# Loading x by halves of the partitions and scoring one group of heads at a time, ahead of a mixture of experts on one core

## The chip, the cores and the metric

The kernel runs on one core of a Trainium2 chip. The metric is the time of one execution on the device in microseconds (us); smaller is better. The time before is the median of three executions.

## The reference

Two parts follow one another. The first is a cross attention between 512 tokens and 32 state rows, for 8 batches of 8 heads of width 64; the second is a mixture of 8 experts over the 544 rows of 512 numbers that each batch then has.

```python
scores = scale * np.matmul(x, state.transpose(0, 1, 3, 2))     # x (8,8,512,64), state (8,8,32,64)
a = softmax(scores);   xread = np.matmul(a, state)             # tokens read the states
scores2 = scale * np.matmul(state, x.transpose(0, 1, 3, 2))
a2 = softmax(scores2); sread = np.matmul(a2, x)                # states read the tokens
x = concatenate([xread, sread], axis=2)                        # then heads side by side: (8, 544, 512)
logits = x @ w_gate;  local_gate = sigmoid(x @ w_local)
# in a sequence, a row takes the expert of the row before it where local_gate >= 0.5,
# and its own best expert otherwise; the first row takes its own
h = np.maximum(x[b, s] @ w1[e], 0.0)                           # w1 (8, 512, 1024)
out[b, s] = p[e] * (h @ w2[e])                                 # w2 (8, 1024, 512), p the softmax of the logits
```

All numbers are float32.

## The kernel before, in words

The 512 tokens of a batch are one "unit", computed whole with the expert of the batch's first token; the state rows and the tokens that need another expert are done in small tiles beside it. A unit is two large products (w1, then w2). Each is taken as seven products of half-size blocks in place of eight (`seven`), so it needs sums of blocks: `first_sum` (`fs0` to `fs3`) adds quarters of w1 (tiles a11, a12, a21, a22), `column_sum` (`cs0` to `cs3`) adds quarters of the unit's tokens, `second_sum` adds quarters of w2 (tiles c). In the first product of a unit, block product 1 needs a11 and the tokens; product 5 is next and needs `fs0`, the sum of a21 and a22; product 6 needs `fs1`.

The attention of batches 0 and 1 runs ahead of the first unit, in the "head". The attention of batches 2 to 7 is cut into steps that are issued between the block products of the units, at numbered ticks (`FLOW`; the functions in `BESIDE` add the leftovers of batches 0 and 1, `GROUPS` the ticks of the routing). The order in the head is written out by hand in the string `HEAD`: one name after another is issued, each engine works its own instructions in that order, and an instruction that waits holds up all behind it on its engine.

A name is a step, a batch and, in most, a group of heads u (0 or 1: group 0 lies on partitions 0 to 63 of the transposed x, group 1 on partitions 64 to 127). The steps that matter here, with their engines:

- `sc` (`scores`, line 321, TensorE): the scores of a batch, eight products with one result bank for each group. `mx` (329, VectorE) is their maximum over the tokens, `nb` (333, GpSimd) its scaled negative, `et` (337, ScalarE) the exponents for the states' reads.
- `tr` (348, VectorE) turns the scores of a group in 32x32 blocks, `mo` (351, VectorE) is the maximum over the states, `sb` (358, GpSimd) subtracts it, `ex` (362, ScalarE) takes exponents, `zh` (369, GpSimd) and `zs` (372, VectorE) sum them, `zi` (377, VectorE) inverts, `ml` (381, GpSimd) multiplies, `tb` (385, VectorE) turns back.
- `tu`, `ec`, `sr`, `iv`, `st`, `rt`, `sl`, `sk`: the states' reads and their logits. `ga`, `gl`: the gates of the states.
- `lg` (436, TensorE) and `lt` (440, VectorE): the logits of the tokens of a batch. `fe` (547 to 553, VectorE): the first token's expert. `vv` (450, TensorE), `xr` and `xd` (459, 462): the tokens' reads, which are the unit's input.
- `kpN` issues N matmuls on zeros into a spare bank.

All loads go through one queue, SyncE's. Its order at the start is: x of batch 0, the other states, the gate weights, x of batch 1, then token-major x of batch 0 (`load_n`), the states again, `load_n` of batch 1, and x and `load_n` of batch 2. The transposed x of a batch is 1 MB in two loads of 512 KB (`load_t`, line 293); each brings two of the four k blocks of all 128 partitions:

```python
x = self.new(self.pools[b]["xp"], f"x_t{h}", (b,), [P, KT // 2, S])
self.nc.sync.dma_start(out=x..., in_=self.xt[b][:, h * D * 2:(h + 1) * D * 2])
```

`fe0` ends with `work.load(0, 0)` (line 839): SyncE waits there for the expert's number and then issues the four quarters of w1, 512 KB each, in the order a11, a21, a22, a12. The four quarters of w2 follow when the memory of the head is free.

Of the kernel before, what the change touches and what calls it, by code (L numbers as in the profile page):

```python
# [18 lines left out]
P = 128  # L19
B, H, S, N, DH = 8, 8, 512, 32, 64  # L20
D = H * DH
# [4 lines left out]
KT = D // P  # L26
FK = F // P
G = 2
# [75 lines left out]
class Banks:  # L104

    def __init__(self, tc, n):
        self.tc, self.ctx = tc, ExitStack()
        self.open(n)
# [8 lines left out]
class Slots:  # L117


    def __init__(self, pool):  # L120
# [17 lines left out]


HEAD = """  # L140
sc0 kp1 tr01 kp2 tr00 mo01 sc1 mo00 sb01 mx01 kp3 sb00 mx11 ex01 kp7 tr11 zh01 ex00 mx00 ga zs01 zh00 mx10 nb0 zi01
et01 zs00 ml01 tr10 et00 tu01 zi00 mo10 nb1 ml00 gl tb01 ec01 sb10 tu00 tb00 et10 mo11 lg0 ec00 sb11 lt0 et11 vv0 fe0
ex10 iv1 sr0 ex11 iv0 xd03 xr02 zh11 xr00 xd01 tu10 zh10 st0 zs11 tu11 zi11 ec10 cs0 ml11 zs10 ec11 zi10 rt0 sr1 ml10
tb11 sl0 st1 kp2 sk0 tb10 cs2 vv1 rt1 cs1 xr10 xr13 fs0 fs1
"""


BESIDE = """
1 lg1 lt1 cs3 fe1 fs3 fs2 xr12 / 2 ze / 3 xr11 / 4 sl1 sk1 / 6 wr12 wr13 / 7 wr10 wr11 / 8 ws0 / 10 ws1 / 11 wr00 wr01 /
12 wr02 wr03  # L150
"""


# [4 lines left out]
"""  # L158
FIRST, PERIOD = 2, 14
PER = 28  # L160
GROUPS = {(0, 2): (5, 8, 9, 11, 13, 14, 15), (2, 4): (57, 60, 61, 61, 64, 65, 67),
          (4, 8): (103, 105, 106, 107, 110, 111, 112)}
ONES = 18, 19, 21, 22, 24, 25, 27, 28, 29

# [1 line left out]
class Attention:  # L166


    def __init__(self, ctx, head, tc, xn, xt, st, stt, wgl, wgs, lt, xts, rows, work):
        nc = self.nc = tc.nc  # L170
        self.xn, self.xt, self.lt, self.xts, self.rows, self.work = xn, xt, lt, xts, rows, work
        self.wg, self.wh = wgs[:, 0], wgs[:, 1]
        self.ctx = ctx.enter_context(ExitStack())

        def pool(name, bufs, of=self.ctx, **more):
            return of.enter_context(tc.tile_pool(name=name, bufs=bufs, **more))

        right = dict(side="right")
        once = pool("once", 1, **right)
        self.tp, self.late = pool("tp", 1, **right), pool("late", 2, **right)  # L180
        self.sm = pool("sm", 3, **right)
        later = dict(xp=pool("xp", 1, **right), wk=pool("wk", 4, **right), tp=self.tp, late=self.late,
                     sp=pool("sp", 2, space=PSUM, **right))
        self.sp = later["sp"]
        self.p = pool("p", 3, space=PSUM, **right)
        first = dict(xp=pool("hx", 2, head), wk=pool("hw", 4, head), tp=pool("ht", 2, head), late=pool("hl", 2, head),
                     sp=later["sp"])
        second = dict(first, late=self.late, sp=pool("hs", 2, head, space=PSUM))
        self.pools = [first, second] + [later] * (B - 2)
        self.of = {}  # L190


        stt = stt.rearrange("p (b k n) -> p b k n", b=B, k=KT)
        self.sttc = [once.tile([P, n, KT, N], F32, name=f"sttc{i}") for i, n in enumerate((1, B - 1))]
        nc.scalar.dma_start(out=self.sttc[0], in_=stt[:, :1])
        for h in range(2):
            self.load_t(0, h)
        self.states_of = once.tile([P, B * G * DH], F32, name="states_of")
        nc.sync.dma_start(out=self.sttc[1], in_=stt[:, 1:])
        nc.sync.dma_start(out=wgs.rearrange("p w k e -> p (w k e)"), in_=wgl)  # L200
        for h in range(2):
            self.load_t(1, h)
        self.load_n(0)
        nc.sync.dma_start(out=self.states_of, in_=st)
        self.load_n(1)
        for h in range(2):
            self.load_t(2, h)
        self.load_n(2)


        self.gl = once.tile([P, B, G, SQ], F32, name="gl")
        self.zh = [once.tile([P, A, N // 2 + 1], F32, name=f"zh{i}") for i in range(2)]
        self.z2 = [once.tile([P, G, 2], F32, name=f"z2{i}") for i in range(4)]
        self.parity = 0
        self.zero = once.tile([P, 512], BF16, name="zero")
        nc.vector.memset(self.zero, 0.0)

        warm = once.tile([1, 1], F32, name="warm")
        nc.vector.memset(warm, 0.0)
        nc.scalar.activation(warm, warm, Act.Exp)  # L220
# [65 lines left out]
    def first_expert(self, b):  # L286
        self.route.first_experts(b, b + 1)
        if b == 0:
            self.work.load(0, 0)

    def load_t(self, b, h):
        x = self.new(self.pools[b]["xp"], f"x_t{h}", (b,), [P, KT // 2, S])
        self.nc.sync.dma_start(out=x.rearrange("p k s -> p (k s)"), in_=self.xt[b][:, h * D * 2:(h + 1) * D * 2])

    def load_n(self, b):
        x = self.new(self.pools[b]["xp"], "x_n", (b,), [P, SC, G, KT, DH])
# [16 lines left out]
        for u, w in enumerate(self.ws):  # L313
            self.nc.scalar.copy(self.gl[:, :, u, :E + 1], w[:, :B * (E + 1)].rearrange("p (b e) -> p b e", b=B))

    def scores(self, b):
        s = [self.new(self.pools[b]["sp"], "s", (b, u), [P, S], tag="s") for u in range(G)]
        for k in range(KT):
            for u in range(G):
                r = slice(64 * u, 64 * u + 64)  # L320
                self.nc.tensor.matmul(s[u][32 * k:32 * k + 32, :], lhsT=self.states(b)[r, k, :],  # L321
                                      rhs=self.get(f"x_t{k // 2}", b)[r, k % 2, :], start=True, stop=True)
        self.new(self.sm, "nb", (b,), [P, G])
        self.new(self.sm, "i2", (b,), [P, G])
        self.new(self.sm, "m1", (b,), [P, G, A])
        self.new(self.sm, "z1", (b,), [P, G, A])
# [478 lines left out]
class Experts:  # L805
# [72 lines left out]
    def at(self, tick, do, *args):  # L878
        self.todo.setdefault(tick, []).append(lambda: do(*args))
# [10 lines left out]
    def run(self, start):  # L890
# [286 lines left out]
        start.flow(at)  # L1177
        for (b0, b1), ticks in GROUPS.items():
            self.steps(route.choose(start.bank, b0, b1), *ticks)
        tick = max(max(t) for t in GROUPS.values()) + 1  # L1180
        at(tick, tiles_begin)
# [100 lines left out]
```

## The time and the profile before

| | |
|---|---|
| time, median of 3 (lowest to highest) | 499.7 us (499.7 to 500.77) |
| the profiled execution: its time, its span | 498.75 us, 497.0 us |
| granted TensorE clock, mean | 0.995 |
| TensorE busy with matmuls | 484.2 us, 97% of the span |
| VectorE, ScalarE, GpSimd busy | 273.4, 160.8, 76.7 us |
| moved by DMA | 115.66 MB, mean 233 GB/s |
| first block product of unit 0 | 27.77 us after the span's start |
| second one, from which TensorE runs on | 30.98 us |

The views used are the page, the chain of waits (followed back from the last instruction), the timeline, TensorE's waits, and tables of short stretches of time. In a timeline row the columns are start, length, engine, line, operation, output and inputs, shapes, count, and in brackets the idle time before it with what ended it. "SPq" is SyncE's queue, whose rows are the issuing of a transfer and not the transfer.

### The profile page before, as it was taken

What the parts mean: (1) busy time and instruction counts of PE and PEld (TensorE: products, weight loads), DVE (VectorE), ACT (ScalarE), POOL (GpSimd) and SP (SyncE); (2) the same over time, 40 slices, a digit from 0 to 9 for tenths busy, and PEclk for the clock granted to TensorE, in tenths of its full rate; (3) what the DMA queues carried; (4) which work ended last, traced back from release to release, by engine and by line L of the source; (5) the groups of instructions that cost most, each with busy time, mean ns of one, the idle gap of its engine ahead of it and who ended that gap; (6) DMA issues with size and microseconds to landing.
All of it is one profiled execution on the core that took longest, in us unless ns stands there. A gap on an engine that the chain in (4) does not pass through costs nothing.

```text
span 497.0 us, 9994 instructions
## 1 busy us (share of the span) xinstructions
PE 484.2 (97%) x4006; PEld 391.5 (79%) x4008; DVE 273.4 (55%) x540; ACT 160.8 (32%) x334; POOL 76.7 (15%) x100
## 2 busy tenths in 40 slices
PE   8889999999999999999999999999999999999994
PEld 2568787887878778888888888888888888888883
DVE  4879984576956878165565934073342633435211
ACT  2633334354343534434213322222122321223210
POOL 6602331121121312200000200000101000000000
PEclk9899999999999999999999999999999999999999
DMA  8877572826839074442809975893999569693411
GB/s 310 342 285 241 191 304 86 290 99 222 335 130 341 21 274 181 163 140 87 294 25 327 399 260 197 320 384 115 404 349 344 200 231 395 258 337 156 171 51 49
DMA packets 40479, 115.66 MB, mean 233 GB/s; under 512 B 7764, under 2 KB 8152, under 8 KB 36200
## 3 DMA queue, kind: packets, MB, share of 16 engines
q1 hardware_dynamic: 39704, 113.76, 62.4%
q0 software_dynamic: 576, 1.12, 0.6%
q8 instruction: 33, 0.54, 0.5%
q14 instruction: 22, 0.18, 0.1%
q10 hardware_dynamic: 144, 0.07, 0.1%
HBM read 97.10 MB, written 17.89 MB: 231 GB/s over the span
## 4 chain that ended last, share of the span: by engine, by line
PE 93%; DMA 3%; DVE 1%; SPq 1%; POOL 0%; issue 0%; DVEq 0%; POOLq 0%
PE ps L1100 23%; PE ps L1054 22%; PE sum L1054 17%; PE sum L1100 16%; PE ps L970 3%; PE ps L957 3%; PE s L321 1%; DMA x_t<-in_xt_dram 1%; DMA a<-in_w_dram 1%; PE p L404 1%; PE p L391 1%; PE s L450 1%; PE p L436 1%; POOL e L381 0%; DVE nb L329 0%; SPq L839 0%
## 5 line engine op out<-in xcount | busy, mean ns | idle before, releaser
L1054 PE MATMUL ps<-x,a 128*128 128x256 f32 x384 | 92.0, 382 | 0.0
L1054 PE MATMUL sum<-xs,a 128*128 128x256 f32 x384 | 91.5, 381 | 0.0
L1054 PEld LDWEIGHTS ps<-x,a 128*128 128x128 f32 x384 | 71.7, 190 | 14.5 <-issue 5.4
L1054 PEld LDWEIGHTS sum<-xs,a 128*128 128x128 f32 x384 | 72.3, 190 | 11.1 <-issue 1.4
L1100 PE MATMUL ps<-c,h 128*128 128x256 f32 x264 | 63.4, 383 | 0.0
L1100 PE MATMUL ps<-c,hs 128*128 128x256 f32 x256 | 60.7, 380 | 0.0
L1100 PE MATMUL sum<-c,h 128*128 128x256 f32 x248 | 58.6, 379 | 0.0
L1100 PEld LDWEIGHTS ps<-c,h 128*128 128x128 f32 x264 | 49.1, 190 | 11.1 <-issue 5.0
L1100 PEld LDWEIGHTS ps<-c,hs 128*128 128x128 f32 x256 | 48.5, 190 | 6.6
L1100 PEld LDWEIGHTS sum<-c,h 128*128 128x128 f32 x248 | 47.1, 190 | 6.4
L849 DVE TENSOR_TENSOR c<-c,c 128x1024 f32<-128x1024 f32 x32 | 40.4, 1296 | 1.5 <-DMA c<-in_w_dram 1.3
L849 DVE TENSOR_TENSOR a<-a,a 128x1024 f32<-128x1024 f32 x32 | 39.6, 1274 | 2.8 <-DMA a<-in_w_dram 2.5
L849 DVE TENSOR_TENSOR h<-s,s 128x512 f32<-128x512 f32 x16 | 11.0, 687 | 44.0 <-ACT s L1083 43.9
L1083 ACT COPY s<-sum 128x512 f32<-128x512 f32 x32 | 18.7, 585 | 41.3 <-PE sum L1054 39.4
L849 DVE TENSOR_TENSOR xs<-x 128x512 f32<-128x512 f32 x16 | 10.8, 678 | 38.3 <-DMA x<-xts 38.3
L922 POOL DMA_INDIRECT xgt<-rows,state x9 | 9.9, 1102 | 139.0 <-DMA ct<-in_w_dram 74.7
L990 ACT COPY sum<-ps 128x512 f32<-128x512 f32 (+1 forms) x32 | 14.9, 465 | 50.2 <-PE ps L1100 26.1
L1054 PE MATMUL ps<-xs,a 128*128 128x256 f32 x128 | 30.4, 381 | 0.6 <-DVE a L849 0.6
L1100 PE MATMUL sum<-c,hs 128*128 128x256 f32 x128 | 30.7, 382 | 0.0
L1104 ACT ACTIVATE s<-sum,prob 128x256 f32<-128x256 f32 x32 | 15.1, 473 | 43.7 <-PE sum L1100 42.4
L1054 PEld LDWEIGHTS ps<-xs,a 128*128 128x128 f32 x128 | 24.2, 190 | 4.1 <-DVE a L849 0.9
L358 POOL TENSOR_TENSOR e<-e,m 128x512 f32<-128x512 f32 x16 | 19.0, 1188 | 53.4 <-DVE m L351 53.4
(187 smaller groups left out, 555.1 us busy)
## 6 DMA issues: line engine op xcount, KB each, us to landing
at<-in_w_dram SPq DMA_DIRECT2D x18, 1024.0 KB
ct<-in_w_dram SPq DMA_DIRECT2D x18, 1024.0 KB
a<-in_w_dram SPq DMA_DIRECT2D x32, 512.0 KB
c<-in_w_dram SPq DMA_DIRECT2D x32, 512.0 KB
x_t<-in_xt_dram SPq DMA_DIRECT2D x16, 512.0 KB
x_n<-in_xn_dram SPq DMA_DIRECT2D x8, 1024.0 KB
out_dram<-y SPq DMA_DIRECT2D x31, 256.0 KB
xts<-xr SPq DMA_DIRECT2D x28, 256.0 KB
```

The costliest lines, as they stand in the source:

```text
L321: self.nc.tensor.matmul(s[u][32 * k:32 * k + 32, :], lhsT=self.states(b)[r, k, :], rhs=self.get(f"x_t{k // 2}", b)[r, k % 2, :], start=Tru ...
L358: self.nc.gpsimd.tensor_tensor(e1, e1, self.each("m1", b, u), op=Alu.subtract)
L391: self.nc.tensor.transpose(t[:, q], self.get("e2", b, u)[:, q], self.route.ident)
L849: self.nc.vector.tensor_tensor(out, a, b, op=op)
L922: nc.gpsimd.indirect_dma_start(out=to.rearrange("p k x -> p (k x)"), out_offset=None, in_=rows.rearrange("n q x -> (n q) x"), in_offset=ba ...
L957: nc.tensor.matmul(hps[SQ * g:SQ * g + SQ, :], lhsT=self.x_t[:, j, :], rhs=a[:, j, :, g], start=(j == 0), stop=(j == KT - 1))
L970: nc.tensor.matmul(yps[SQ * g:SQ * g + SQ, :], lhsT=self.h[:, m, :], rhs=self.ct[:, 2 * m // FK, g // 2, m % (FK // 2), g % 2 * P:g % 2 * ...
L990: nc.scalar.copy(y, x)
L1054: nc.tensor.matmul(to[:, m * width:m * width + width], lhsT=w[:, j, f:f + P], rhs=x[:, j, :], start=begin and m == 0 and j == 0, stop=(m = ...
L1083: return lambda t: nc.scalar.copy(to, t)
L1100: nc.tensor.matmul(to, lhsT=x[:, m, n * P:n * P + P], rhs=w[:, m, :], start=begin and m == 0, stop=(m == FK // 2 - 1), skip_group_check=True)
L1104: return lambda t: nc.scalar.activation(to, t, Act.Copy, scale=p)
```

## The change

- `load_t` loads the transposed x of a batch into one tile, and its two loads bring 64 partitions each, all four k blocks, in place of all partitions and two k blocks. This holds for all eight batches.
- `scores` can be issued for one group: `sc00` needs partitions 0 to 63 alone, `sc01` the rest. Only batch 0 is issued so.
- The three loads of x of batch 2 (2 MB) go from the start of the queue to behind the four quarters of w1 for unit 0.
- `HEAD` has another order. Batch 0's group 0 comes first, both its maxima (`mx01`, `mx00`) stand ahead of batch 1's `tr11` and `mx11`, and the fill matmuls stand elsewhere. `sl0 sk0 vv1 rt1 fs0 fs1 cs2 xr10` and some more go from the end of `HEAD` to tick 1 of `BESIDE`, which is issued between block products 1 and 5; `fs3` now stands ahead of `lt1`.
- A step of the routing at ticks 64 and 65 goes to 63.

```diff
 HEAD = """
-sc0 kp1 tr01 kp2 tr00 mo01 sc1 mo00 sb01 mx01 kp3 sb00 mx11 ex01 kp7 tr11 zh01 ex00 mx00 ga zs01 zh00 mx10 nb0 zi01
-et01 zs00 ml01 tr10 et00 tu01 zi00 mo10 nb1 ml00 gl tb01 ec01 sb10 tu00 tb00 et10 mo11 lg0 ec00 sb11 lt0 et11 vv0 fe0
-ex10 iv1 sr0 ex11 iv0 xd03 xr02 zh11 xr00 xd01 tu10 zh10 st0 zs11 tu11 zi11 ec10 cs0 ml11 zs10 ec11 zi10 rt0 sr1 ml10
-tb11 sl0 st1 kp2 sk0 tb10 cs2 vv1 rt1 cs1 xr10 xr13 fs0 fs1
+sc00 sc01 tr00 mo00 kp7 tr01 sb00 mo01 kp1 sc1 ex00 mx01 sb01 mx00 ga zh00 tr11 ex01 mx11 nb0 kp3 zh01 et00 mx10 gl
+zs01 nb1 zi01 et11 zs00 tu00 ml01 tr10 et01 zi00 kp2 mo11 ml00 et10 tu01 tb01 sb11 ec00 tb00 ec01 mo10 lg0 ex11 vv0
+sb10 lt0 fe0 zh11 tu11 xr02 iv0 iv1 tu10 xd03 ec11 zs11 ex10 kp2 xd01 xr00 sr0 zh10 zi11 ec10 ml11 zs10 sr1 st0 zi10
+ml10 tb11 st1 cs0 rt0 cs1 tb10
 """
 BESIDE = """
-1 lg1 lt1 cs3 fe1 fs3 fs2 xr12 / 2 ze / 3 xr11 / 4 sl1 sk1 / 6 wr12 wr13 / 7 wr10 wr11 / ...
+1 sl0 sk0 vv1 lg1 rt1 fs0 fs1 fs3 lt1 cs3 fs2 cs2 fe1 xr10 xr12 / 2 ze / 3 xr11 / 4 sl1 sk1 xr13 / 6 wr10 wr12 / 7 wr11 wr13 / ...
 """
-GROUPS = {..., (2, 4): (57, 60, 61, 61, 64, 65, 67),
+GROUPS = {..., (2, 4): (57, 60, 61, 61, 63, 63, 67),
...
         self.load_n(1)
-        for h in range(2):
-            self.load_t(2, h)
-        self.load_n(2)
...
         if b == 0:
             self.work.load(0, 0)
+            for h in range(2):
+                self.load_t(2, h)
+            self.load_n(2)

     def load_t(self, b, h):
-        x = self.new(self.pools[b]["xp"], f"x_t{h}", (b,), [P, KT // 2, S])
-        self.nc.sync.dma_start(out=x.rearrange("p k s -> p (k s)"), in_=self.xt[b][:, h * D * 2:(h + 1) * D * 2])
+        x = self.new(self.pools[b]["xp"], "x_t", (b,), [P, KT, S])
+        r = slice(64 * h, 64 * h + 64)
+        self.nc.sync.dma_start(out=x[r].rearrange("p k s -> p (k s)"), in_=self.xt[b][r])

-    def scores(self, b):
+    def scores(self, b, *us):
         s = [self.new(self.pools[b]["sp"], "s", (b, u), [P, S], tag="s") for u in range(G)]
         for k in range(KT):
-            for u in range(G):
+            for u in us or range(G):
                 r = slice(64 * u, 64 * u + 64)
                 self.nc.tensor.matmul(s[u][32 * k:32 * k + 32, :], lhsT=self.states(b)[r, k, :],
-                                      rhs=self.get(f"x_t{k // 2}", b)[r, k % 2, :], start=True, stop=True)
+                                      rhs=self.get("x_t", b)[r, k, :], start=True, stop=True)
+        if us == (1,):
+            return
```

More of the change, by code (lines that the diff above doesn't have):

```diff
@@ L140 @@
 HEAD = """
-sc0 kp1 tr01 kp2 tr00 mo01 sc1 mo00 sb01 mx01 kp3 sb00 mx11 ex01 kp7 tr11 zh01 ex00 mx00 ga zs01 zh00 mx10 nb0 zi01
-et01 zs00 ml01 tr10 et00 tu01 zi00 mo10 nb1 ml00 gl tb01 ec01 sb10 tu00 tb00 et10 mo11 lg0 ec00 sb11 lt0 et11 vv0 fe0
-ex10 iv1 sr0 ex11 iv0 xd03 xr02 zh11 xr00 xd01 tu10 zh10 st0 zs11 tu11 zi11 ec10 cs0 ml11 zs10 ec11 zi10 rt0 sr1 ml10
-tb11 sl0 st1 kp2 sk0 tb10 cs2 vv1 rt1 cs1 xr10 xr13 fs0 fs1
+sc00 sc01 tr00 mo00 kp7 tr01 sb00 mo01 kp1 sc1 ex00 mx01 sb01 mx00 ga zh00 tr11 ex01 mx11 nb0 kp3 zh01 et00 mx10 gl
+zs01 nb1 zi01 et11 zs00 tu00 ml01 tr10 et01 zi00 kp2 mo11 ml00 et10 tu01 tb01 sb11 ec00 tb00 ec01 mo10 lg0 ex11 vv0
+sb10 lt0 fe0 zh11 tu11 xr02 iv0 iv1 tu10 xd03 ec11 zs11 ex10 kp2 xd01 xr00 sr0 zh10 zi11 ec10 ml11 zs10 sr1 st0 zi10
+ml10 tb11 st1 cs0 rt0 cs1 tb10
 """
 BESIDE = """
-1 lg1 lt1 cs3 fe1 fs3 fs2 xr12 / 2 ze / 3 xr11 / 4 sl1 sk1 / 6 wr12 wr13 / 7 wr10 wr11 / 8 ws0 / 10 ws1 / 11 wr00 wr01 /
-12 wr02 wr03
+1 sl0 sk0 vv1 lg1 rt1 fs0 fs1 fs3 lt1 cs3 fs2 cs2 fe1 xr10 xr12 / 2 ze / 3 xr11 / 4 sl1 sk1 xr13 / 6 wr10 wr12 /
+7 wr11 wr13 / 8 ws0 / 10 ws1 / 11 wr00 wr01 / 12 wr02 wr03
 """
@@ L160 @@
 PER = 28
-GROUPS = {(0, 2): (5, 8, 9, 11, 13, 14, 15), (2, 4): (57, 60, 61, 61, 64, 65, 67),
+GROUPS = {(0, 2): (5, 8, 9, 11, 13, 14, 15), (2, 4): (57, 60, 61, 61, 63, 63, 67),
           (4, 8): (103, 105, 106, 107, 110, 111, 112)}
```

## The prediction

> **What bounds the kernel now.** I read the page first, then TensorE's waits, then the chain of waits over the first 33 us (its longest pieces), then the timeline and 1 us stretches there.
>
> ```profile
> span 497.0 us, 9994 instructions
> ...
> PE 484.2 (97%) x4006; PEld 391.5 (79%) x4008; DVE 273.4 (55%) x540; ACT 160.8 (32%) x334; POOL 76.7 (15%) x100
> ```
>
> ```profile
> PE s L450 <- DVE a L385: 1.1, 1, 1.1
> PE ps L1054 <- DVE a L849: 0.6, 1, 0.6
> ```
>
> TensorE is busy for 97% of the span. The second fence holds all its waits after 27 us: one at the head's last reads (line 450), and one in the units (line 1054), 0.6 us on VectorE's sum of w1 quarters. So what the units cost does not depend on this change as long as their weights and x are there in time. What can move is the moment from which TensorE runs without waits, and for that the chain of the head is the view (start, length, what):
>
> ```profile
> 3.46 6.93 DMA x_t<-in_xt_dram
> 10.44 1.11 PE s L321 x8
> 14.71 0.94 POOL e L381
> 15.94 1.01 POOL e L381
> 17.84 1.11 PE p L436 x16
> 21.48 1.22 SPq L839
> 22.89 6.72 DMA a<-in_w_dram
> 29.70 1.24 DVE a L849
> 30.98 1.99 PE ps L1054 x8
> ```
>
> It reads: x of batch 1 lands at 10.39 and its scores end at 11.55; after steps of both batches on VectorE and GpSimd, batch 0's logits run at 17.84; then come the first expert and the issue of w1; its third quarter, a22, lands at 29.61, `fs0` starts at 29.70 and block product 5 at 30.98. Each us by which `fs0` comes sooner is a us of the whole time, if TensorE's earlier work is out of the way by then.
>
> **The change part by part.** VectorE's rows around batch 1's scores:
>
> ```profile
> 7.93 1.31 DVE L348 STREAM_TRANSPOSE e<-s 128x512 f32<-128x512 f32 x2 [1.67 <-PE s L321]
> 9.17 1.24 DVE L351 TENSOR_REDUCE m<-e 128x16 f32<-128x512 f32 x2
> 10.32 0.68 DVE L329 TENSOR_REDUCE nb<-s 128x1 f32<-128x512 f32 x1
> 11.57 0.69 DVE L329 TENSOR_REDUCE nb<-s 128x1 f32<-128x512 f32 x1 [0.56 <-PE s L321]
> 12.18 0.70 DVE L348 STREAM_TRANSPOSE e<-s 128x512 f32<-128x512 f32 x1
> 12.81 0.65 DVE L329 TENSOR_REDUCE nb<-s 128x1 f32<-128x512 f32 x1
> 13.38 0.41 DVE L372 TENSOR_REDUCE z<-zh 128x16 f32<-128x272 f32 x1
> ```
>
> *Scores of batch 0 by groups.* VectorE began at 7.93, when the scores of both groups were through. With `sc00` on the first load, group 0 is through one block of eight matmuls sooner; such a block took 1.11 in the chain, so VectorE begins about 1.1 us sooner, near 6.8. But it doesn't keep that: its next six steps, both turns (1.31), both maxima over the states (1.24), `mx01` (0.68) and `mx00` (0.65), sum to 3.9 and end near 10.7, and then `tr11` waits for batch 1's scores, which still end at 11.55 if that x lands as before. What is late next is that load. The gain is one step: `mx00` (12.81 to 13.38, 0.57 from start to start) is now done in the wait. VectorE's other steps from there to batch 0's logits are the same ones, with `mo11` and `mo10` exchanged, and GpSimd's two products (14.71 and 15.94 in the chain) wait on VectorE's inverses, which come sooner with it. I take 0.6. The low end is 0 (GpSimd holds the old pace), the high end 1.1 (all of the earlier begin).
>
> *The x loads by halves of the partitions.* There are still two loads of 512 KB a batch. No transfer of this size in the trace fills 64 partitions, so the price is bounded by the nearest rows. The last two columns are the share of the DMA engines that is busy and GB/s:
>
> ```profile
> 3.00:4.00 1.00, 1.00 (x4) 0.32 (x3) 0.09 (x1) 0.00 (x0) 1.00 (x7) 1.00 0.81 270
> 7.00:8.00 1.00, 1.00 (x13) 0.11 (x2) 0.07 (x1) 0.00 (x0) 0.00 (x0) 1.00 1.05 415
> 11.00:12.00 1.00, 1.00 (x11) 0.31 (x4) 0.44 (x2) 0.63 (x2) 1.00 (x2) 1.00 0.99 410
> 20.00:21.00 1.00, 1.00 (x25) 0.00 (x0) 0.62 (x6) 0.05 (x1) 0.88 (x2) 0.66 0.70 295
> 21.00:22.00 1.00, 1.00 (x66) 0.81 (x61) 0.58 (x1) 0.62 (x2) 0.55 (x1) 1.00 0.31 70
> 35.00:36.00 1.00, 1.00 (x6) 0.90 (x5) 1.00 (x1) 0.87 (x2) 0.00 (x0) 1.00 0.19 75
> ```
>
> At 7 to 8 us the transposed x passes, at 11 to 12, after its landing, the loads behind it, among them token-major x in rows of 8 KB, as long as the rows of the new loads: 415 and 410. Row length makes no difference, so at that rate a half takes 512 KB / 415 = 1.26 us as before: price 0. The low end is a gain: at 3 to 4 us only 270 GB/s flowed, and if half as many, longer rows get the engines going sooner, x of batch 1 lands up to 1 us sooner. The high end is half the rate, in case what limits a transfer is how much of the partitions' width it reaches: four halves ahead of batch 1's scores at 1.26 more each make 5.0, of which up to 2 are covered by the slow start. So +3 to +5. I take 0, by the 410 row, the nearest in row length, and keep both ends.
>
> [...]
>
> *Batch 2's x behind w1.* The old queue was busy until past 21 (295, then 70 GB/s), just beyond the issue of w1 (20.93, quoted next); 2 MB less at 410 GB/s empties it near 16. So w1 meets an empty queue: 0 to 1.0 us gained (at most the thin stretch 21 to 22); a loss is excluded, as nothing new stands ahead of w1.
>
> ```profile
> 20.93 0.35 SPq L839 DMA_DIRECT2D a<-in_w_dram  x1
> ...
> 36.71 1.09 PE L321 MATMUL s<-x_t,sttc 64*32 64x512 f32 x16
> ...
> 47.56 3.33 DVE L849 TENSOR_TENSOR c<-c,c 128x1024 f32<-128x1024 f32 x2
> ```
>
> From 20.93 to 29.61 pass 8.7 us for three quarters, 1.5 MB, far more than the old queue explains; I take the middle, 0.5. SyncE issues three more loads behind w1, and w2 stands behind 2 MB: its last bytes passed at 35 to 36 (75 GB/s) and come about 5 us later, near 40. VectorE takes w2 at 47.56: 7 us of cover, price 0. Batch 2's scores read x at 36.71, with block product 7 queued behind them. w1 is all in near 30, 1 MB more at 410 GB/s near 33: about 3 us of cover, price 0. With halves at half rate it is 36 to 37, and then up to 1 us of stall.
>
> *The tail of the head behind block product 1.* TensorE's `sl0`, `vv1` and `lg1` stand between products 1 and 5 now:
>
> ```profile
> 23.55 1.15 PE L404 MATMUL p<-x_n,e 128*32 128x64 f32 x64 [0.24 <-ACT e L395]
> 24.83 0.39 PE L424 MATMUL p<-wgs,rt 128*32 128x9 f32 x8
> ...
> 26.60 0.62 PE L450 MATMUL s<-a,states_of 32*32 32x512 f32 x2 [1.05 <-DVE a L385]
> ...
> 27.77 1.99 PE L1054 MATMUL ps<-x,a 128*128 128x256 f32 x8
> 29.70 0.64 PE L436 MATMUL p<-a,gl 128*32 128x128 f32 x16
> ```
>
> Product 1 takes 1.99, `sl0` 0.39, `vv1` 1.2 (26.60 to 27.77), `lg1` 0.64: 4.2 in all. Product 5 is due near 29.9, so product 1 must start by 25.7. It needs a11, the first third of those 8.7 us, near 24 before and near 23 now, and TensorE, whose `sr1` ended at 24.7 and ends near 24. Cover 1.5 us, price 0; if it is gone, up to 0.5. `fs3` needs a12, the fourth quarter, and stands ahead of `lt1`, `cs3` and `fs2` on VectorE; they feed products 7 and later, 5 us behind product 5: price 0. The routing steps move by a tick or two, and TensorE has no wait on them: 0. The fill matmuls change the granted clock under `lg0`, which took 1.11 where `lg1` took 0.64: up to 0.4 either way, taken as 0.
>
> **The sum.** 0.6 + 0.5 = 1.1 us less. Against the profiled execution's 498.75 that is 497.65; that execution lies 0.95 below the median, so against the median of 499.7 it is **498.6 us**.
>
> **The rivals.**
> - *Slower: halves at half rate.* x of batch 1 lands at 13.4 to 15.4 in place of 10.39, and VectorE's chain from `tr11` on moves with it: +3 to +5, less the 1.1, plus 0 to 1 at batch 2's scores: 501.6 to 504.6, most likely 503. For it: nothing in the trace shows a half loaded at full rate. Against it: nothing shows one at half rate, and row length is free. It decides as soon as that load is over 1.1 us late.
> - *No change.* The first expert is known sooner, but a22 lands no sooner (its quarters came slowly, at 1.5 MB in 8.7 us, for a reason of their own), or TensorE is not through with `vv1` in time: 499.2 to 500.2.
> - *More.* The slow start shortens, x of batch 1 lands up to 1 us sooner and VectorE's wait of 0.9 ahead of `tr11` goes: 2.0 in all, 497.7.
>
> **How the numbers follow.** Forecast case 0.35 (its own range 497.9 to 499.3), half rate 0.34, no change 0.14, more 0.17. A measurement of this kernel tells about 0.3%, 1.5 us, from no change. Faster (below 498.2): a third of the forecast case and nearly all of "more", 0.28. Slower (above 501.2): 0.34. Within: the rest, 0.38. The range 497.0 to 503.8 leaves out the top of the half-rate case and the end of "more", under 0.2.
>
> **What would show it.** In the changed profile: VectorE's first turn near 6.8; batch 1's scores from 10.4 (right) or from 13 on (half rate); about 410 or about 210 GB/s while x of batch 1 passes; batch 0's logits near 17.2, the issue of w1 near 20.3, `fs0` near 28.6; no wait at batch 2's scores. The prediction is wrong if an x load of 64 partitions takes longer than 1.26 us, or if `fs0` doesn't follow the first expert.

## The result, and the profile after

| | before | after |
|---|---|---|
| time, median (lowest to highest) of 6 runs each | 499.53 us (498.73 to 500.77) | 502.94 us (501.99 to 503.58) |
| the profiled execution: time, span | 498.75 us, 497.0 us | 502.86 us, 501.1 us |
| batch 1's score products that need the last load of its x (TensorE) | 10.44 us | 14.75 us |
| logits of batch 0, `lg0` | 17.84 | 21.55 |
| issue of w1 | 20.93 | 24.88 |
| `fs0` | 29.70 | 33.91 |
| block product 5 | 30.98 | 35.20 |

The change made the kernel slower: the ratio is 1.0068, with a 95% interval of 1.0051 to 1.0085. The page after, first the span, then the busy times:

```profile
span 501.1 us, 9999 instructions
...
PE 484.0 (97%) x4008; PEld 391.3 (78%) x4008; DVE 274.4 (55%) x540; ACT 160.8 (32%) x334; POOL 75.8 (15%) x100
```

TensorE's busy time is as before within 0.2 us, the others' within 1.0. The span grew by 4.1 us, so the loss is waiting. The chain of waits after (start, length, what) says where:

```profile
3.62 11.09 DMA x_t<-in_xt_dram
...
14.75 0.33 PE s L322
...
15.93 0.72 DVE e L351
...
18.60 2.06 POOL e L384 x2
...
21.55 0.68 PE p L439 x16
...
24.88 0.35 SPq L842
...
25.97 7.85 DMA a<-in_w_dram
...
33.91 1.24 DVE a L852
...
35.20 1.99 PE ps L1057 x8
```

It is the chain of before, but its first piece takes 11.09 us in place of 6.93. (In both kernels part of batch 1's scores runs sooner, on the first load of its x; what counts here are the products behind the last load.) The pieces, before and after: these scores, 4.31 us later; from there to `lg0` 7.40 and 6.80; from `lg0` to the issue of w1 3.09 and 3.33; from the issue to `fs0` 8.77 and 9.03; from `fs0` to product 5 1.28 and 1.29. Together 4.31 - 0.60 + 0.24 + 0.26 + 0.01 = 4.22 us, which is the shift of product 5, and the span grew by 4.1. Behind product 5 little changes: 0.4 us are lost at batch 2's scores (they took 1.09 us from 36.71 before and take 1.49 from 40.92 now), and about 0.5 is won back by the end. VectorE's waiting in the timeline after, with idle time and releaser in brackets:

```profile
7.43 0.72 DVE L351 STREAM_TRANSPOSE e<-s 128x512 f32<-128x512 f32 x1 [1.17 <-PE s L322]
...
11.06 1.28 DVE L332 TENSOR_REDUCE nb<-s 128x1 f32<-128x512 f32 x2
15.93 0.72 DVE L351 STREAM_TRANSPOSE e<-s 128x512 f32<-128x512 f32 x1 [3.60 <-PE s L322]
```

VectorE ends both maxima of batch 0 near 12.3 and then sits idle for 3.60 us until `tr11` has its scores; it waited 0.56 us there before. The 1 us stretches show the loads themselves; the last two columns are the busy share of the 16 DMA engines and GB/s:

```profile
7.00:8.00 1.00, 0.37 (x4) 0.00 (x0) 0.56 (x1) 0.00 (x0) 0.00 (x0) 1.00 0.95 204
...
11.00:12.00 1.00, 1.00 (x4) 0.30 (x2) 1.00 (x3) 0.00 (x0) 0.78 (x1) 0.50 0.95 221
```

The engines are as busy as before (0.95, against 1.05 and 0.99) and move half as much (204 and 221 GB/s, against 415 and 410). They are not idle; each byte takes them twice as long.

### The profile page after: what moved, and what is told of

Same layout as the page of the kernel before. It is cut to its first block, busy times and chain, and to the rows that moved or that the text cites. A ratio compares the mean times of both kernels' runs of the same rounds, so it can differ in the third digit from the quotient of the medians.

```text
span 501.1 us, 9999 instructions
## 1 busy us (share of the span) xinstructions
PE 484.0 (97%) x4008; PEld 391.3 (78%) x4008; DVE 274.4 (55%) x540; ACT 160.8 (32%) x334; POOL 75.8 (15%) x100
## 4 chain that ended last, share of the span: by engine, by line
PE 92%; DMA 4%; DVE 1%; SPq 1%; POOL 0%; issue 0%; DVEq 0%; POOLq 0%
PE ps L1103 23%; PE ps L1057 22%; PE sum L1057 17%; PE sum L1103 16%; PE ps L973 3%; PE ps L960 3%; DMA x_t<-in_xt_dram 2%; DMA a<-in_w_dram 2%; PE s L322 2%; PE p L407 1%; PE p L394 1%; PE s L453 1%; PE p L439 1%; POOL e L384 0%; SPq L294 0%; PE p L427 0%
## 5 line engine op out<-in xcount | busy, mean ns | idle before, releaser
L982 POOL DMA_INDIRECT out_dram<-yt,row x9 | 10.0, 1106 | 114.4 <-DVE yt L977 99.5
```

The costliest lines, as they stand in the source:

```text
L982: put = nc.gpsimd.indirect_dma_start(out=out.rearrange("n (q x) -> (n q) x", q=Q), out_offset=at, in_=y, in_offset=None, bounds_check=NT * ...
```

## The experiments

All times are medians; each group of kernels ran on one chip beside the kernel before, whose median was 499.19 us for the first four, 499.02 for the next four, 498.74 for the next three, 499.0 for the last. "Scores" is the start of those score products of batch 1 that need the last load of its x, "w1" the issue of w1, "fs0" the start of `fs0`, in us of the profiled execution. There is one profiled execution of each kernel, so these columns have no interval.

| kernel | time | ratio to before (95%) | scores | lg0 | w1 | fs0 |
|---|---|---|---|---|---|---|
| `halves_alone` | 508.8 | 1.0211 (1.0164 to 1.0257) | 14.49 | 22.81 | 25.65 | 38.38 |
| `rest_alone` | 497.31 | 0.9967 (0.9947 to 0.9987) | 10.57 | 17.34 | 20.67 | 28.07 |
| `strided` | 497.13 | 0.9959 (0.9943 to 0.9975) | 10.14 | 17.02 | 20.36 | 28.80 |
| `whole` | 496.67 | 0.9947 (0.9930 to 0.9964) | 9.96 | 16.81 | 20.15 | 28.31 |
| `first_only` | 499.87 | 1.0032 (1.0016 to 1.0047) | 12.79 | 19.61 | 22.95 | 31.23 |
| `first_two` | 501.99 | 1.0058 (1.0037 to 1.0080) | 14.85 | 21.67 | 25.20 | 33.66 |
| `two_queues` | 502.36 | 1.0072 (1.0055 to 1.0088) | 15.33 | 22.13 | 25.47 | 33.87 |
| `old_order` | 497.64 | 0.9973 (0.9963 to 0.9983) | 10.05 | 17.51 | 20.34 | 28.64 |
| `x2_front` | 497.45 | 0.9974 (0.9963 to 0.9984) | 10.06 | 16.95 | 20.28 | 29.52 |
| `whole_again` | 496.94 | 0.9973 (0.9954 to 0.9991) | 11.21 | 18.03 | 21.36 | 29.64 |
| `middle` | 499.35 | 1.0007 (0.9992 to 1.0022) | 12.54 | 19.34 | 22.68 | 29.81 |
| `mo_late` | 496.42 | 0.9945 (0.9930 to 0.9960) | 10.00 | 16.86 | 19.52 | 26.80 |

**`halves_alone`: the kernel before with the loads by halves and nothing else.**

```diff
-        self.nc.sync.dma_start(out=x..., in_=self.xt[b][:, h * D * 2:(h + 1) * D * 2])
+        self.nc.sync.dma_start(out=x[r]..., in_=self.xt[b][r])   # r = 64 partitions
```

> The kernel before with one edit: x by halves of the partitions (order of the head, whole scores and batch 2's x at the front of the queue as before). Theory 'reach' (a transfer to 64 neighbouring partitions runs at half rate): GB/s near 205 while x of batches 0, 1 and 2 passes, batch 1's scores from about 14.7 us, w1 issued near 25.5, and as batch 2's x (5 us instead of 2.5) now stands ahead of w1, fs0 6 to 7 us later than before: 505.5 to 506.5 us. Rival 'order' (the new order of the head costs the time): as before, 499.5. Rival 'rows' (64 rows of 8 KB are slow because they are few or long): as 'reach' here.

The sign was as expected, and the loss larger than the 6 to 7 us expected: 9.6. Batch 1's scores came 4.05 us later than in the kernel before. The rest is seen in TensorE's waits:

```profile
PE s L322 <- DMA x_t<-in_xt_dram: 4.8, 4, 2.1
PE p L451 <- issue: 3.6, 1, 3.6
PE p L405 <- issue: 1.3, 1, 1.3
```

Two waits of 3.6 and 1.3 us stand in `vv0` and in the states' reads (`sr`), which before had none of this size. "issue" means that the profile names no releaser. They are not waits for a late load of what these steps read: both fall in the middle of a step, behind products that had already read the same tensors (`vv0` began at 23.39 and stopped at 25.13, `sr1` began at 33.15 and stopped at 34.20). The transfers of the trace point at TensorE's own instructions. Of its matmuls, weight loads and semaphore steps exactly 256 are on record between the two waits, and on the queue that brings instructions a block of 16 KB landed at 27.29 and another at 34.13, each 1.4 us before TensorE went on; that TensorE waited for them is read from this order alone. The first such block passed at 17.33 in the kernel before and at 26.16 here. Why it came so late was not tested; x of batch 2 by halves was passing until 25.7 us, from 21 on at 205 to 229 GB/s.

**`rest_alone`: the changed kernel with the old kind of load, two k blocks of all 128 partitions.**

```diff
-        self.nc.sync.dma_start(out=x[r]..., in_=self.xt[b][r])
+        self.nc.sync.dma_start(out=x[:, 2*h:2*h+2]..., in_=self.xt[b][:, h*D*2:(h+1)*D*2])
```

> The changed kernel with one edit: each x load brings two k blocks of all 128 partitions again, into the one tile; everything else of the change stays (sc00 then waits for both loads). 'Reach' and 'rows': 410 GB/s, batch 1's scores from 10.4, batch 0's logits near 17.2 (0.6 sooner than before), w1 issued near 20.4, time 498.5 to 499.5. 'Order': 503.

497.31, better than the 498.5 to 499.5 expected. The rest of the change gains 1.9 us, and the loads by halves cost 502.94 - 497.31 = 5.6 us in the changed kernel. The two runs were beside different runs of the kernel before (499.53 and 499.19).

**`strided`: the same 64 rows of 8 KB in each load, but every second partition.**

```diff
-        self.nc.sync.dma_start(out=x[r]..., in_=self.xt[b][r])
+        self.nc.sync.dma_start(out=x[h::2]..., in_=self.xt[b][h::2])
```

> The changed kernel with one edit: the first x load brings the even partitions, the second the odd ones: still 64 rows of 8 KB in each load, but spread over the whole width. 'Reach': full rate, 410 GB/s, 498.5 to 499.5. 'Rows': half rate, 205 GB/s, 503.

The stretch from 7 to 8 us in `strided`:

```profile
7.00:8.00 1.00, 1.00 (x18) 0.31 (x4) 0.49 (x1) 0.00 (x0) 0.00 (x0) 1.00 0.98 412
```

412 GB/s in place of 204, with as many partitions, as long rows and as many loads. What halves the rate is neither the count of 64 partitions nor the row length, but which 64 they are. Scores of one group can't begin on half of such a load, and yet the kernel is 5.8 us faster than the changed one and below its expected range.

**`whole`: one load of 1 MB a batch.**

```diff
+        if h == 0:
+            self.nc.sync.dma_start(out=x..., in_=self.xt[b])
```

> The changed kernel with one edit: x of a batch in one load of 1 MB, 128 rows of 8 KB. 'Reach': full rate, batch 1's scores from 10.4 or a little sooner, 498.5 to 499.5. 'Rows', if it is the length that counts: half rate, 503; if it is the number: full rate.

The stretch from 7 to 8 us, and two pieces of the chain of `whole`:

```profile
7.00:8.00 1.00, 1.00 (x12) 0.41 (x5) 0.68 (x1) 0.00 (x0) 0.00 (x0) 1.00 1.02 434
```

```profile
21.24 6.98 DMA a<-in_w_dram
...
28.31 1.24 DVE a L852
```

434 GB/s, and w1's third quarter takes 6.98 us after the last issue on the chain where it took 7.85 in the changed kernel. `whole` beats both kernels and its expected range: 496.67. Part of the 6.98 and 7.85 has another cause, told under batch 2's x below.

**`first_only` and `first_two`: halves for batch 0 alone, and for batches 0 and 1; the others whole.**

```diff
+        if b == 0:          # first_two: if b < 2
             r = slice(64 * h, 64 * h + 64)
             self.nc.sync.dma_start(out=x[r]..., in_=self.xt[b][r])
+        elif h == 0:
+            self.nc.sync.dma_start(out=x..., in_=self.xt[b])
```

> The changed kernel, only batch 0's x by halves of the partitions, the other batches' x in one load of 1 MB. 'Reach' by dose: two of the four halves ahead of batch 1's scores at half rate, so these start near 12.2 us (9.96 with all loads whole, 14.7 with both batches by halves), fs0 2.3 later than with whole loads, 498.5 to 499.5 us. Rival, that the early group 0 pays for the slower load: batch 0's first turn on VectorE at 7.4, as with whole loads at 7.3, so nothing to win; it would need under 497.

> The changed kernel, x of batches 0 and 1 by halves, of batches 2 to 7 whole. Theory: the slow loads also hurt once more behind w1, where batch 2's halves share the rings with the last quarters of w1 (w1's issue to fs0 took 9.0 us in the changed kernel against 7.4 to 8.4 in the three kernels without halves). Then batch 1's scores start at 14.7 as in the changed kernel, but fs0 follows the issue of w1 by 7.4 to 8.4: 501.3 to 502.3 us. Rival, that all of the loss lies ahead of batch 1's scores: 502.9, as the changed kernel.

`first_only` was expected at 498.5 to 499.5 and gave 499.87. By the trace's landings x of batch 1 was in at 11.87 (in `whole` at 9.83), 2.0 us later for two halves, near the 2.2 expected. But its scores started only at 12.79, because eight fill matmuls stood ahead of them, most of them at half the clock. The row before them in TensorE's timeline, and theirs, without a wait in brackets:

```profile
10.01 2.85 PE L281 MATMUL p<-zero 128*128 128x512 bf16 x8
12.79 1.09 PE L325 MATMUL s<-x_t,sttc 64*32 64x512 f32 x16
```

The same eight took 1.90 us in `whole`. TensorE had waited 1.36 us for the second half of batch 0's x, until 8.32, and from 8.6 to 12.0 the granted clock was 0.50; that the wait lowered it was not tested. `first_two` is within its range. It is 0.95 us under the changed kernel, but their ratios to the kernel before are not separated (1.0037 to 1.0080 against 1.0051 to 1.0085). From the issue of w1 to `fs0` it took 8.46 us against 9.03. So the halves of batches 0 and 1, ahead of batch 1's scores, carry nearly all of the loss; what those of batch 2 behind w1 add is some tenths in the traces and not shown in the times.

**`two_queues`: as `first_two`, the second half on ScalarE's queue.**

```diff
-            self.nc.sync.dma_start(out=x[r]..., in_=self.xt[b][r])
+            (self.nc.scalar if h else self.nc.sync).dma_start(out=x[r]..., in_=self.xt[b][r])
```

> As first_two, but the second half (partitions 64 to 127) of batches 0 and 1 is issued on ScalarE's queue, so both halves are under way at once. If halves are slow only because one follows the other in one queue: 410 GB/s, batch 1's scores near 10.2, 496.5 to 497.5 us. [...]

Two stretches of `two_queues`:

```profile
7.00:8.00 1.00, 0.00 (x0) 0.00 (x0) 0.94 (x2) 0.00 (x0) 0.00 (x0) 0.64 1.06 223
...
9.00:10.00 1.00, 0.97 (x8) 0.20 (x8) 0.00 (x0) 0.37 (x1) 0.60 (x1) 0.50 0.93 192
```

223 and 192 GB/s in place of 410, and batch 1's scores at 15.33 in place of 10.2. The two halves do not add up to the full rate when they come from two queues. (ScalarE's queue has one small load in the other kernels too: the 64 KB of batch 0's states.)

**`old_order`: `whole` with the old `HEAD`, `BESIDE` and `GROUPS`.**

> Whole loads and batch 2's x behind w1, but the head's order, tick 1 and the routing tick of the kernel before: batch 0's scores unsplit. It parts the gain of the whole loads with the new order (496.7) into order and the rest. If the moved loads carry it: w1's issue to fs0 7.4 to 8.4 (8.8 before), 497.2 to 498.2. If the order carries it: 498.7 to 499.5.

497.64. From batch 1's scores to `lg0` it takes 17.51 - 10.05 = 7.46 us, in `whole` 16.81 - 9.96 = 6.85: the new order is worth 0.6 there. In the times it is not separated: the ratio to the kernel before is 0.9973 here, 0.9947 in `whole` and 0.9973 in `whole_again`, the same kernel as `whole`.

**`x2_front` and `whole_again`: `whole` with the three loads of batch 2 back at the start of the queue, and `whole` once more beside it.**

> Whole loads and the new order of the head, but batch 2's x back at the front of the queue. Against whole_again it prices the move of batch 2's x by itself. If the old queue held w1 up: w1's issue to fs0 8.8 or more against 8.2, fs0 0.6 to 1.4 us later than with x behind w1, 497.3 to 498.1 us. If w1 is slow for a reason of its own: 496.7, no difference.

> The kernel of the run 'whole' once more, beside x2_front and in more rounds: the changed kernel with x of a batch in one load of 1 MB. 496.4 to 497.2 us.

497.45 and 496.94, with intervals that overlap. In the traces the issue of w1 to `fs0` takes 9.24 us with batch 2's x in front, 8.28 without. So the move is worth 0.5 in the times (not separated) and 1.0 in the two traces. Both traces are of executions well above their kernels' medians: 499.77 us of `x2_front`, the longest of its 12, and 498.55 of `whole_again`, 1.6 above. In the latter x of batch 1 was in at 10.01, but the eight fills ahead of its scores took 3.00 us, as slow as in `first_only`, and the scores started at 11.21. The clock rows of that execution say 1.00 there, but its first record of the clock stands at 10.5; no half-rate load was ahead, so why it was slow stays open.

**`middle`: the first load brings partitions 32 to 95, then 0 to 31 and 96 to 127 follow.**

```diff
+        for r in (slice(0, 32), slice(96, 128)) if h else (slice(32, 96),):
+            self.nc.sync.dma_start(out=x[r]..., in_=self.xt[b][r])
```

> The changed kernel, but the first x load of a batch brings partitions 32 to 95, the second and third 0 to 31 and 96 to 127. If any 64 neighbouring partitions are half the width: about 205 GB/s all the time, batch 1's scores near 14.7 us, 502 to 503.5. [...]

Two stretches of `middle`:

```profile
8.00:9.00 1.00, 1.00 (x11) 0.29 (x4) 0.97 (x2) 0.00 (x0) 0.00 (x0) 1.00 1.04 430
9.00:10.00 1.00, 1.00 (x6) 0.41 (x5) 0.97 (x3) 0.00 (x0) 0.74 (x1) 1.00 1.18 287
```

The rate changes within a batch, between 430 GB/s and 211 to 287, and the last load of batch 1's x is used at 12.54, not near 14.7, between `whole` (9.96) and the changed kernel (14.75): half of the bytes at half the rate, about half of the delay. So 64 neighbouring partitions are not slow as such: 32 to 95 pass fast, the outer quarters slow. Why some partitions pass at half the rate was not shown. The runs give the rates alone: 204 and 221 GB/s for halves from 64 and from 0 (the changed kernel), 412 for every second partition (`strided`), 430 and 211 to 287 here.

**`mo_late`: `whole` with `mo10`, `sb10` and `zh11` behind `fe0`.** In the kernels of the new order the way from `lg0` to the issue of w1 was 3.3 us, not 3.1 (3.5 in `first_two`, where `lg0` ran at a granted clock of 0.50). Two steps of `fe0` on VectorE had grown. These rows are of `whole`, VectorE's first and GpSimd's second:

```profile
18.05 0.33 DVE L551 TENSOR_TENSOR near<-lt,first 1x8 f32<-1x8 f32 x1
18.41 0.66 DVE L552 SCALAR_TENSOR_TENSOR near<-near,iof 1x8 f32<-1x8 f32 x1
```

```profile
17.31 1.05 POOL L361 TENSOR_TENSOR e<-e,m 128x512 f32<-128x512 f32 x1 [0.39 <-DVE m L354]
18.32 0.74 POOL L372 TENSOR_TENSOR zh<-e 128x256 f32<-128x256 f32 x1
```

Eight numbers took 0.66 us, and each of the two steps ends when GpSimd's product beside it ends: 18.38 with 18.36, 19.07 with 19.06.

```diff
-... tb00 ec01 mo10 lg0 ex11 vv0 sb10 lt0 fe0 zh11 ...
+... tb00 ec01 lg0 ex11 vv0 lt0 fe0 mo10 sb10 zh11 ...
```

> The best kernel so far (one load of 1 MB per batch, new order) with one step of the head's order moved: mo10 (VectorE), and with it sb10 and zh11 (GpSimd), stand behind fe0. Everything is computed as before. In that kernel the two steps of fe0 that read two tensors took 0.33 and 0.66 us (18.05 and 18.41) and ended when GpSimd's products beside them ended (18.36 and 19.06); in the kernel before, with GpSimd idle beside them, they took 0.15 each. Theory 'a two-input step of VectorE waits out GpSimd's product': with GpSimd idle both take 0.15, the distance from batch 0's logits to the issue of w1 falls from 3.34 to 2.6 to 2.8 us, and the issue comes near 19.5 in place of 20.15. Rival 'these steps are slow in the new order for another reason (their operands)': 0.33 and 0.66 again, the distance stays 3.3. For the total: fs0 follows the issue, 496.0 to 496.4, if batch 1's later steps (sb10 starts some 2 us later than at 17.31) are still through before product 5, whose TensorE wait was 1.3 us; 496.7 or more if lg1 then ends behind fs0.

The same two steps in `mo_late`, where GpSimd is idle from 16.97 to 19.47:

```profile
18.10 0.15 DVE L551 TENSOR_TENSOR near<-lt,first 1x8 f32<-1x8 f32 x1
18.29 0.15 DVE L552 SCALAR_TENSOR_TENSOR near<-near,iof 1x8 f32<-1x8 f32 x1
```

From `lg0` to the issue of w1 it is 19.52 - 16.86 = 2.66 us, as the theory had it; the rival falls. `fs0` starts at 26.80, 1.5 us sooner than in `whole`. Only 0.6 of that is the shorter way to the issue of w1; 0.9 is w1 itself, which took 7.28 us in place of 8.16 for the reason told under batch 2's x below. Product 5 comes only 1.0 us sooner (28.60), because it now stands right behind `lg1`. The chain of `mo_late`:

```profile
28.02 0.57 PE p L439 x16
28.60 1.93 PE ps L1057 x8
```

So the tail of batch 1's attention has become the bound of the head. The time, 496.42, is the lowest of all, but not separated from `whole`'s 496.67 (0.9930 to 0.9960 against 0.9930 to 0.9964). What the rows show is that the two steps end with GpSimd's products in `whole` and take 0.15 us each with GpSimd idle in `mo_late`; why was not shown.

## Why the prediction was wrong

*The price of the loads by halves.* This is the step that failed. The prediction took 0, chose it by the 410 GB/s row of rows of 8 KB, and kept +5, at half the rate, as the high end, an assumption for which it had no row. Row length had been the wrong likeness: `strided` has the same row length, count of partitions and loads as the change and runs at 412 GB/s, the change at 204. What counts is which partitions a load covers, and no load of the trace before could show that, as all large ones covered all 128. Measured, x of batch 1 came 4.31 us later, in the rival's 3 to 5. The rival's 503 is the result (502.94), but that it fits so well is in part luck: it took the forecast's 1.1 off, of which 0.6 came, and the profiled execution before lies 0.8 below its median, so that profile to profile 4.1 were lost and by the medians 3.4.

*The scores by groups and the order.* 0.6 was predicted and 0.60 measured (7.40 to 6.80), and 0.61 between `old_order` and `whole`. VectorE's first turn began at 7.43, not near 6.8: `sc00` started at 6.03, where the scores before started at 5.56, since its half of x came at 197 and 205 GB/s (4 to 6 us, before 338 and 412). As VectorE waited 3.60 us later on, that cost nothing. In the kernels with one load a batch `sc00` can't run early at all, and the gain is there still, so the early group did not bring it; the order did, as the step said (`mx00` done in the wait). In `whole`, VectorE's first turn even began at 7.32, sooner than in the changed kernel.

*Batch 2's x behind w1.* 0.5 was predicted. With full-width loads it is 0.5 in the times (not separated) and 1.0 in the two traces. In the changed kernel it was turned into a loss of 0.26 between the issue and `fs0`. A loss had been excluded, since nothing new stands ahead of w1. But loads behind it pass beside it: of the packets that began from 33 to 35 us, 46 were rows of 8 KB, batch 2's, and 6 rows of 4 KB, w1's, and the rate is about half.

```profile
33.00:34.00 1.00, 0.25 (x10) 0.00 (x0) 0.09 (x1) 0.87 (x2) 0.00 (x0) 1.00 1.02 176
34.00:35.00 1.00, 0.00 (x0) 0.00 (x0) 1.00 (x1) 0.00 (x0) 0.00 (x0) 1.00 1.04 225
```

These are stretches of the changed kernel; `first_two` moved 418 and 426 GB/s in the same two, which there too stand about eight to ten us behind the issue of w1. Up to eight us behind the issue both had moved the same, 2.24 and 2.25 MB.

The landings in the trace say more. Each load of x and w1 lands in 16 parts. In the changed kernel 15 parts of w1's third quarter were in at 32.14, 7.3 us behind the issue, and in the kernels with full-width loads behind w1 after 6.7 to 7.5. The last part came at 33.82, 1.7 us after the others. In the other kernels with batch 2's x behind w1 this last part lags too, by 0.8 to 1.4 us, but in `rest_alone` and `mo_late` by less than 0.1, and in `middle` too. These three also have the shortest way from the issue to `fs0` (7.40, 7.28 and 7.13). The lag goes with a block of 16 KB on the queue that brings instructions, which takes about 1 us: where the third quarter's last part lags, the block began 2.0 to 2.8 us before that part landed; in the three others it came later, and the lag, of 0.9 to 2.1 us, begins with the fourth quarter. That the block holds the part up is read from this order alone and was not tested. Of the 0.57 us between the changed kernel and `first_two` about half is the lag, so the halves behind w1 can have cost `fs0` no more than some tenths.

The stall at batch 2's scores, priced at up to 1 us with halves at half rate, came to 0.4: the last part of its second half landed at 41.20, and TensorE loaded the weights of the products that need it at 41.30, 0.4 us into the scores. TensorE's longest waits in the changed kernel do not name it, since the first products were still running:

```profile
PE s L322 <- DMA x_t<-in_xt_dram: 2.3, 3, 1.2
PE ps L1057 <- DVE a L852: 1.9, 1, 1.9
PE ps L1057 <- DMA a<-in_w_dram: 1.4, 1, 1.4
```

*From `lg0` to the issue.* The prediction had no term for it and kept the old 3.1 us (17.2 to 20.3). It grew by 0.24 us, and that is a difference of two: `lg0` took 0.68 in place of 1.11, as the granted clock there was 1.00 in place of 0.50, and from its end the way grew by 0.67, as two steps of `fe0` met GpSimd's products, which `mo_late` showed. The routing steps, moved by a tick or two and priced at 0, show no wait of TensorE.

*The tail of the head behind product 1.* Price 0 was right in the changed kernel: TensorE waited 1.9 us for `fs0` after it. In `mo_late`, where `fs0` comes at 26.80, the cover is gone, as the step warned.

*The fill matmuls.* Taken as 0, with up to 0.4 either way under `lg0`. There 0.4 was gained, though no run shows that the fills did it. Their place mattered more ahead of `sc1`: eight of them held batch 1's scores for 0.9 us after its x was in, in `first_only`, and for 1.2 in the profiled execution of `whole_again`.

## What to carry to other kernels

Before a load is split by partitions, ask which partitions each part covers: here 64 neighbours from 0 or 64 moved at 221 and 204 GB/s, every second partition at 412, and a second queue did not help (223 and 192). A row of the trace prices a new operation only if it is like it in what limits it; when all rows of a trace share a property (here, all 128 partitions), none of them says what happens without it. And an instruction of eight numbers on the critical chain is worth a look at what the neighbouring engine does at that moment.

## What the runs showed of the hardware that was not expected

- Small two-input steps of VectorE (1x8) took 0.33 and 0.66 us beside a GpSimd product (`whole`) and 0.15 us without one (`mo_late`).
- The last of a load's 16 parts can lag: w1's third quarter was in but for one part after 6.7 to 7.5 us, and the last part came 0 to 1.7 us later, which moved `fs0` by as much. In the kernels with batch 2's x behind w1 it lagged where a 16 KB block of instructions had begun 2.0 to 2.8 us before it landed, and not where the block came later.
- TensorE stopped for 3.6 and 1.3 us in `halves_alone`, 256 instructions apart, and went on 1.4 us after a 16 KB block of instructions had landed.
- Eight fill matmuls took 2.85 us in `first_only`, most of them at a granted clock of 0.50, in `whole` 1.90 at 1.00, and in `first_only` stood ahead of scores whose data were there.
